# Wider rows for the first loads of queries and keys, and two more pairs of half sums added before the matrix engine

## The chip, the cores and the metric

The kernel runs on one core of a Trainium2 chip. The metric is device time in microseconds (us), the median over the runs. A separate profiled execution gives the trace, whose times count from the start of its span.

Five engines work side by side, each through its own list of instructions in order: PE (TensorE, matmuls; its weight loads are PEld), DVE (VectorE), ACT (ScalarE), POOL (GpSimd) and SP (SyncE, which here issues most DMAs; ACT issues a few). PE writes to `ps`, the accumulation memory of eight banks; everything else lies in `arena`, the on-chip memory that the kernel divides by hand.

## The reference

Attention in which a query sees only keys of its own cluster, then an MLP mixer over tokens and channels (biases and normalisation layers there are none):

```python
# q, k, v: [4, 8, 768, 64]; centroids: [8, 16, 64]
q_assign = argmax(q_n @ c_n.T); k_assign = argmax(k_n @ c_n.T)   # q_n, k_n, c_n: rows of length 1
mask = q_assign[:, :, :, None] == k_assign[:, :, None, :]
scores = where(mask, 0.125 * q @ k.T, -1e9)
attn = softmax(scores) @ v
x = heads side by side: [4, 768, 512]
xt = x.transpose(0, 2, 1)
u = x + (relu(xt @ w_tok1) @ w_tok2).transpose(0, 2, 1)
out = u + relu(u @ w_ch1) @ w_ch2
```

## The kernel before, in words

The 32 (batch, head) problems are worked as 16 pairs of neighbouring heads, pair 0 to pair 15. For a pair m:

- `load_qk` (pairs 0 to 2) brings q and k on chip, `turn_qk` transposes them on PE into a bank and copies them to `Ts[m % 3]`, twelve rows of 128 tokens: rows 0 to 5 keys, 6 to 11 queries, the two heads on partitions 0 to 63 and 64 to 127. For later pairs `load_qkr`, `part_qk` and `join_qk` do it through transposing DMAs.
- `route` multiplies the rows with the normalised centroids (`cbd`), and DVE finds each token's cluster; the result becomes the mask operand. For pair 0 it is placed directly by eight small operations (lines 1116 to 1141), for the others by way of DRAM (`wdm`).
- `scores` gives twelve chunks: two plain matmuls (one per head), two mask matmuls on top of them in the same banks, and ACT's exponential out of the banks. For pair 0 three chunks' plain matmuls are issued ahead.
- `add_up` adds the exponentials of six key blocks on DVE into two half sums `es[0]`, `es[1]`; where `FOLD[m]` is "V", DVE adds these two as well (one 128x1536 add more).
- `values` multiplies exponentials and v, 16 matmuls for each of six blocks. `sums` multiplies the half sums with ones for the denominators: four matmuls for each half, so eight without the fold and four with it. `sums(m - 1)` runs in the values of pair m.

An fp32 matmul that is no transposition runs as two passes, so the trace shows twice as many.

Before pair 0, `begin` loads centroids, queries and keys, lets PE run `BUSY` warming matmuls on the identity, normalises the centroids on DVE (with one square root on ACT), turns the normalised centroids on PE and copies them to `cbd`. ACT then loads the table of the exponential (line 1005).

After the pairs come the token stage and the channel stage of the mixer, in a fast matrix multiplication with seven products in place of eight; its sums of operands and results are adds on DVE and POOL (line 885), and DVE frees the banks that PE writes. The weights of the mixer are rounded by `weight_round` (lines 1380 to 1397, 31 pieces of up to 512 columns, released at `START + STEP * npiece`) and summed on DVE during the pairs and the token stage, and written to DRAM (`wd`, `wdt`) by SP.

What sets the order: PE's instructions stand as the program adds them. All others are put in order ahead of time by `Program.plan`, a list scheduler with a cost for each operation, due times worked back from PE's order, and times before which an operation is not released (`after`); an operation that names two engines (ACT and DVE for copies) goes to the one that the planner finds free earlier. `more` is added to a transfer's planned time to landing.

Of the kernel before, what the change touches and what calls it, by code (L numbers as in the profile page):

```python
# [29 lines left out]
HJ = NJ // 2  # L30
HS = HJ * P
# [18 lines left out]
GRAIN = 32  # L50
BUSY, HITS_AT = 12, 18.0
CHECK_AT = 532.0
FOLD = "-VVVVVVVVVV-----"

# [7 lines left out]
ISSUE = 0.63  # L62
# [7 lines left out]
SELF = 0.13  # L70
START, STEP = 9, 10

# [651 lines left out]
def kernel(  # L724
# [43 lines left out]
    def buf(kb, shape, dt=F32):  # L768
        return Buf(arena, int(kb * 256), shape, dt)
# [15 lines left out]

    qks = [buf(3 + 6 * i, [2, NJ, 2, D]) for i in range(2)]
    vs = [buf(15 + 3 * i, [2, NJ, D]) for i in range(3)]
# [52 lines left out]
    def bank(*i):  # L840
        return [("ps", n) for n in i]
# [58 lines left out]

    def dma(dst, src, rd, wr, kb, row, after=0.0, queue="SP"):

        q = {"SP": nc.sync, "ACT": nc.scalar, "POOL": nc.gpsimd}[queue]
        return g.add(
            {queue: ISSUE}, lambda e: q.dma_start(dst, src), rd, wr, (kb * 1024, row), after  # L905
        )
# [8 lines left out]
    def load_qk(m, after=0.0, queues=("SP", "SP")):  # L915
        b, hp = divmod(m, H // 2)
        t = qks[m % 2]
        for i, a in ((1, k), (0, q)):
            for h, qu in enumerate(queues):
                dma(  # L920
                    t.ap[:, i, :, h],
                    a[b, 2 * hp + h].rearrange("(p j) d -> p j d", p=P),
                    [], [("qk", m % 2, i, h)] + (t.rows(i, i + 1) if h else []), 192, 256,
                    after, qu,
                )

# [19 lines left out]
    def begin():  # L946
        cen, sq = rt[0], rt[1]
        dma(cen.ap[:, 0:D], centroids.rearrange("h c d -> (h c) d"), [], cen.k(), 32, 256)
        load_qk(0, 0.0, ("SP", "ACT"))
        load_qk(1, 1.0)  # L950
# [49 lines left out]

        g.add({"DVE": 4.0}, norm, cen.k(), sq.k() + nsq.k())
        turn_qk(0, (0, 1, 2), (0, 1))
        turn(ps[:, 7, 0:P], sq.ap[:, 0:P], sq.k(), bank(7))
        turn_qk(0, (0, 1, 2), (2,))
        g.add(
# [29 lines left out]

    def turn_qk(m, banks, parts=range(3)):
        src, T = qks[m % 2], Ts[m % 3]
        for n in parts:
            bk = banks[n]
            for i in range(4):  # L1040
                a, j = divmod(4 * n + i, NJ)
                a = 1 - a
                turn(
                    ps[:, bk, i * P : (i + 1) * P],
                    src.ap[:, a, j].rearrange("p h d -> p (h d)"),
                    [("qk", m % 2, a, 0), ("qk", m % 2, a, 1)] + src.rows(a, a + 1), bank(bk),
                )

            copy(
                T.ap[:, 4 * n : 4 * n + 4].rearrange("p a t -> p (a t)"), ps[:, bk], 512,  # L1050
                bank(bk), T.rows(4 * n, 4 * n + 4),
            )

# [107 lines left out]
    def scores(m):  # L1161
# [166 lines left out]
    def pair(m):  # L1328
# [727 lines left out]
```

## Time and profile before

| | us |
|---|---|
| median of 3 runs | 789.43 |
| lowest, highest | 789.1, 789.65 |
| profiled execution | 789.87 |
| its span | 788.0 |

In a line of the timeline stand start, length, engine, line, operation, what it writes and reads, shape and count; in brackets the idle time of the engine before it and what ended it. A group's length runs from its first start to its last end. In the table of stretches stand, for each engine, busy time and count of instructions; behind them the granted clock of PE, the busy share of the 16 DMA engines and what they moved in GB/s. SPq and ACTq are DMA issues. The shape of a copy is partitions x elements.

### The profile page before, as it was taken

What the parts mean: (1) busy time and instruction counts of PE and PEld (TensorE: products, weight loads), DVE (VectorE), ACT (ScalarE), POOL (GpSimd) and SP (SyncE); (2) the same over time, 40 slices, a digit from 0 to 9 for tenths busy, and PEclk for the clock granted to TensorE, in tenths of its full rate; (3) what the DMA queues carried; (4) which work ended last, traced back from release to release, by engine and by line L of the source; (5) the groups of instructions that cost most, each with busy time, mean ns of one, the idle gap of its engine ahead of it and who ended that gap; (6) DMA issues with size and microseconds to landing.
All of it is one profiled execution on the core that took longest, in us unless ns stands there. A gap on an engine that the chain in (4) does not pass through costs nothing.

```text
span 788.0 us, 15324 instructions
## 1 busy us (share of the span) xinstructions
PE 777.8 (99%) x5975; PEld 463.1 (59%) x5975; DVE 675.2 (86%) x848; ACT 461.4 (59%) x614; POOL 194.1 (25%) x187
## 2 busy tenths in 40 slices
PE   8999999999999999999999999999999999999996
PEld 5666666666666666545555555555555555555554
DVE  6979999999998999999999877999853576799964
ACT  5788888889889875599614368633235204400422
POOL 0000000000000000001274598700285289830000
PEclk9999999999999999999999999999999999999999
DMA  9676668876778953568848999975788744444666
GB/s 249 169 192 180 170 154 221 212 202 178 196 196 215 266 178 128 127 135 202 195 124 253 313 281 266 273 189 132 168 189 177 165 100 101 105 105 102 160 164 161
DMA packets 326576, 143.68 MB, mean 182 GB/s; under 512 B 260192, under 2 KB 322400, under 8 KB 326496
## 3 DMA queue, kind: packets, MB, share of 16 engines
q1 hardware_dynamic: 324128, 141.83, 71.6%
q8 instruction: 49, 0.80, 0.4%
q10 hardware_dynamic: 2368, 0.79, 0.4%
q14 instruction: 31, 0.25, 0.1%
HBM read 91.95 MB, written 28.61 MB: 153 GB/s over the span
## 4 chain that ended last, share of the span: by engine, by line
PE 95%; DVE 3%; DMA 1%; issue 0%; ACT 0%; SPq 0%
PE ps L846 77%; PE ps L1238 18%; DVE arena L885 2%; DMA arena<-in_q_dram 1%; DMA arena<-in_moe_w_ch_dram 0%; ACT arena L865 0%; DVE arena L1384 0%; DVE arena L1390 0%; DVE arena L1387 0%; SPq L905 0%; DVE arena L1380 0%; DVE arena L867 0%; ACT arena L1129 0%
## 5 line engine op out<-in xcount | busy, mean ns | idle before, releaser
L846 PE MATMUL ps<-arena 128*128 128x384 f32 (+5 forms) x2727 | 640.2, 463 | 4.5 <-POOL arena masks.py:199 1.4
L846 PEld LDWEIGHTS ps<-arena 128*128 128x128 f32 (+2 forms) x2343 | 340.1, 184 | 250.3 <-issue 61.6
L885 DVE TENSOR_TENSOR arena<-arena 128x1536 f32<-128x1536 f32 (+6 forms) x340 | 369.9, 1109 | 12.5 <-issue 3.6
L885 POOL TENSOR_TENSOR arena<-arena 128x384 f32<-128x384 f32 x181 | 193.4, 1109 | 501.8 <-DVE arena L885 378.6
L885 DVE TENSOR_TENSOR arena<-ps,arena 128x384 f32<-128x384 f32 (+3 forms) x227 | 189.4, 844 | 78.4 <-PE ps L846 76.0
L875 ACT COPY arena<-arena 128x768 uint16<-128x768 uint16 x221 | 189.2, 955 | 62.6 <-DMA arena<-arena 32.8
L1205 ACT ACTIVATE arena<-ps 128x768 f32<-128x768 f32 x192 | 150.7, 811 | 35.2 <-PE ps L846 33.4
L1238 PE MATMUL ps<-arena 128*32 128x192 f32 (+1 forms) x3248 | 144.9, 335 | 0.0
L1238 PEld LDWEIGHTS ps<-arena 128*32 128x32 f32 x3248 | 103.7, 110 | 44.1 <-issue 15.6
L865 ACT COPY arena<-ps 128x512 f32<-128x512 f32 (+2 forms) x44 | 31.3, 719 | 116.1 <-PE ps L846 114.8
L892 ACT ACTIVATE arena<-arena 128x1152 f32<-128x1152 f32 (+1 forms) x38 | 39.7, 1070 | 51.0 <-DVE arena L885 50.3
L1912 ACT ACTIVATE arena<-arena 128x768 f32<-128x768 f32 x40 | 38.7, 969 | 32.8 <-DMA arena<-in_moe_w_ch_dram 27.1
L846 PEld LDWEIGHTS <-arena 64*128 64x128 bf16 x384 | 19.2, 94 | 24.6 <-issue 0.2
L1390 DVE SCALAR_TENSOR_TENSOR arena<-arena 128x512 f32<-128x512 uint32 (+1 forms) x31 | 21.5, 713 | 0.4
L1384 DVE SCALAR_TENSOR_TENSOR arena<-arena 128x512 uint32<-128x512 uint32 (+1 forms) x31 | 20.9, 695 | 0.3
L1108 ACT ACTIVATE arena<-arena 128x384 bf16<-128x384 f32 x16 | 11.2, 701 | 13.6 <-issue 13.6
L1380 DVE TENSOR_SCALAR arena<-arena 128x512 uint32<-128x512 uint32 (+1 forms) x31 | 13.9, 458 | 4.0 <-DMA arena<-in_moe_w_tok_dram 4.0
L1285 DVE STREAM_TRANSPOSE arena<-ps 128x768 f32<-128x768 f32 x16 | 15.2, 952 | 0.4 <-PE ps L1238 0.4
L1387 DVE TENSOR_SCALAR arena<-arena 128x512 uint32<-128x512 uint32 (+1 forms) x31 | 12.8, 436 | 0.4
L1293 DVE STREAM_TRANSPOSE arena<-ps 128x384 f32<-128x384 f32 x16 | 9.3, 579 | 2.2 <-PE ps L1238 2.0
L1098 DVE STREAM_TRANSPOSE arena<-ps 128x384 f32<-128x384 f32 x16 | 9.1, 571 | 1.8 <-PE ps L846 1.8
L1103 DVE STREAM_TRANSPOSE arena<-arena 128x384 f32<-128x384 f32 x16 | 9.3, 578 | 0.6
(57 smaller groups left out, 47.2 us busy)
## 6 DMA issues: line engine op xcount, KB each, us to landing
arena<-wd SPq DMA_DIRECT2D x196, 192.0 KB, 3.0
wd<-arena SPq DMA_DIRECT2D x84, 224.0 KB, 3.0
arena<-in_moe_w_ch_dram SPq DMA_DIRECT2D x96, 128.0 KB, 3.1
arena<-in_moe_w_ch_dram SPq DMA_DIRECT2D x16, 768.0 KB, 5.3
arena<-in_v_dram SPq DMA_DIRECT2D x16, 384.0 KB, 4.8
out_dram<-arena SPq DMA_DIRECT2D x14, 384.0 KB, 3.5
arena<-in_k_dram SPq DMA_DIRECT2D x13, 384.0 KB, 4.2
arena<-in_q_dram SPq DMA_DIRECT2D x13, 384.0 KB, 4.2
```

Source lines behind the costliest of these rows:

```text
L846: nc.tensor.matmul(dst, lhsT=lhsT, rhs=rhs, start=start, stop=stop, tile_position=pos, is_transpose=tr, skip_group_check=True,)
L865: nc.scalar.copy(out=dst, in_=src)
L875: nc.scalar.copy(out=dst, in_=src)
L885: (nc.vector if e == "DVE" else nc.gpsimd).tensor_tensor(out=dst, in0=a, in1=b, op=op)
L892: nc.scalar.activation(out=dst, in_=src, func=ACT.Relu)
L1205: lambda e, ex=ex, s=s, u=u: nc.scalar.activation(out=ex.ap[:, :, u * HS : (u + 1) * HS], in_=ps[:, 2 * s : 2 * s + 2, 0:HS], func=ACT.Exp ...
L1238: nc.tensor.matmul(dst, lhsT=lhsT, rhs=rhs, start=start, stop=stop, tile_position=pos, skip_group_check=True,)
L1285: lambda: nc.vector.transpose(out=x.ap[:, :, cols].rearrange("p j (c d) -> p c j d", d=32), in_=ps[:, 6:8, 0:HS],),
L1380: vec(lambda: nc.vector.tensor_scalar(out=hh, in0=hi, scalar1=0x07FFFFFF, scalar2=3, op0=ALU.bitwise_and, op1=ALU.logical_shift_left,), f, ...
L1384: vec(lambda: nc.vector.scalar_tensor_tensor(out=TT, in0=hi, scalar=0xC0000000, in1=hh, op0=ALU.bitwise_and, op1=ALU.bitwise_or), 0.14 + 0 ...
L1390: vec(lambda: nc.vector.scalar_tensor_tensor(out=ll, in0=lo, scalar=float(2.0**-52), in1=hh.bitcast(F32), op0=ALU.mult, op1=ALU.mult,), 0. ...
L1912: lambda e, i=i, func=func, bias=bias, n=n, hi=hi: nc.scalar.activation(out=hi, in_=hi, func=func, bias=bias, accum_out=wsum.ap[:, i, n : ...
```

## The change

- `load_qk` loads both heads of q, or of k, in one DMA of 384 KB: the layout on chip becomes [q or k, head, row, 64], so that each partition gets 1536 bytes in one piece per head, where it got six pieces of 256 bytes. For pair 0 the keys go by ACT's queue and the queries by SP's; so far each queue had one head of both. The centroids' DMA is issued after the queries on SP.
- `turn_qk` turns two rows of one head at a time (64 values each of token rows 2i and 2i + 1), four parts of three turns in place of three parts of four. Each part is copied by two copies of 64x384 (even rows and odd rows), which put the head on its partitions.
- In pair 0 the first two parts of pair 1 are turned ahead of the three plain chunks, the other two after them.
- `BUSY` from 12 to 9, `START` from 9 to 7, some planned costs (`norm`, the centroids' landing).
- `FOLD`: pairs 11 and 12 get the third add.

In the order that the planner gives the changed kernel, pair 0's eight copies stand seven on ACT and one on DVE, pair 1's six and two, pair 2's five and three; the reduction of line 1019 and its two scalings stand behind the two `cbd` copies, where they stood ahead of them; all else on PE stands as before but for the edits named.

```diff
-BUSY, HITS_AT = 12, 18.0
+BUSY, HITS_AT = 9, 18.0
-FOLD = "-VVVVVVVVVV-----"
+FOLD = "-VVVVVVVVVVVV---"
-START, STEP = 9, 10
+START, STEP = 7, 10
...
-    qks = [buf(3 + 6 * i, [2, NJ, 2, D]) for i in range(2)]
+    qks = [buf(3 + 6 * i, [2, 2, NJ, D]) for i in range(2)]
...
-        for i, a in ((1, k), (0, q)):
-            for h, qu in enumerate(queues):
-                dma(
-                    t.ap[:, i, :, h],
-                    a[b, 2 * hp + h].rearrange("(p j) d -> p j d", p=P),
-                    [], [("qk", m % 2, i, h)] + (t.rows(i, i + 1) if h else []), 192, 256,
-                    after, qu,
-                )
+        for (i, a), qu in zip(((1, k), (0, q)), queues):
+            dma(
+                t.ap[:, i].rearrange("p h j d -> p h (j d)"),
+                a[b, 2 * hp : 2 * hp + 2].rearrange("h (p j) d -> p h (j d)", p=P),
+                [], t.rows(i, i + 1), 384, 1536, after, qu,
+            )
...
-        dma(cen.ap[:, 0:D], centroids.rearrange("h c d -> (h c) d"), [], cen.k(), 32, 256)
-        load_qk(0, 0.0, ("SP", "ACT"))
+        dma(
+            cen.ap[:, 0:D], centroids.rearrange("h c d -> (h c) d"), [], cen.k(), 32, 256,
+            more=-1.7,
+        )
+        load_qk(0, 0.0, ("ACT", "SP"))
...
-        g.add({"DVE": 4.0}, norm, cen.k(), sq.k() + nsq.k())
-        turn_qk(0, (0, 1, 2), (0, 1))
+        g.add({"DVE": 3.0}, norm, cen.k(), sq.k() + nsq.k())
+        turn_qk(0, (0, 1, 2, 4))
         turn(ps[:, 7, 0:P], sq.ap[:, 0:P], sq.k(), bank(7))
-        turn_qk(0, (0, 1, 2), (2,))
...
-    def turn_qk(m, banks, parts=range(3)):
+    def turn_qk(m, banks, parts=range(4)):
...
-            for i in range(4):
-                a, j = divmod(4 * n + i, NJ)
-                a = 1 - a
+            a, h = divmod(n, 2)
+            for i in range(HJ):
                 turn(
                     ps[:, bk, i * P : (i + 1) * P],
-                    src.ap[:, a, j].rearrange("p h d -> p (h d)"),
-                    [("qk", m % 2, a, 0), ("qk", m % 2, a, 1)] + src.rows(a, a + 1), bank(bk),
+                    src.ap[:, 1 - a, h, 2 * i : 2 * i + 2].rearrange("p j d -> p (j d)"),
+                    src.rows(1 - a, 2 - a), bank(bk),
                 )
-            copy(
-                T.ap[:, 4 * n : 4 * n + 4].rearrange("p a t -> p (a t)"), ps[:, bk], 512,
-                bank(bk), T.rows(4 * n, 4 * n + 4),
-            )
+            for j in range(2):
+                copy(
+                    T.ap[D * h : D * h + D, NJ * a + j : NJ * (a + 1) : 2],
+                    ps[D * j : D * j + D, bk, 0:HS].rearrange("p (i t) -> p i t", t=P), HS,
+                    bank(bk), sum((T.rows(NJ * a + i, NJ * a + i + 1) for i in range(j, NJ, 2)), []),
+                )
...
         ahead = 3 if m == 0 else 0
+        if m == 0:
+            turn_qk(1, (7, 6), (0, 1))
         for n in range(ahead):
             plain(n)
         if m == 0:
-            turn_qk(1, (7, 6, 7))
+            turn_qk(1, (0, 0, 7, 6), (2, 3))
...
-                turn_qk(2, (1, 2, 3))
+                turn_qk(2, (1, 2, 3, 4))
```

More of the change, by code (lines that the diff above doesn't have):

```diff
@@ L899, in vec, with dma @@
         return g.add({"DVE": c - 0.08}, lambda e: fn(), rd, wr, after=after, early=early)
-    def dma(dst, src, rd, wr, kb, row, after=0.0, queue="SP"):
+    def dma(dst, src, rd, wr, kb, row, after=0.0, queue="SP", more=0.0):
         q = {"SP": nc.sync, "ACT": nc.scalar, "POOL": nc.gpsimd}[queue]
         return g.add(
-            {queue: ISSUE}, lambda e: q.dma_start(dst, src), rd, wr, (kb * 1024, row), after
+            {queue: ISSUE}, lambda e: q.dma_start(dst, src), rd, wr, (kb * 1024, row), after,
+            more=more,
         )
```

## The prediction

> **What bounds the kernel now.** First the page: its totals, VectorE's (DVE's) busy tenths in 40 slices of 19.7 us, and the chain of waits that ended last.
>
> ```profile
> span 788.0 us, 15324 instructions
> PE 777.8 (99%) x5975; PEld 463.1 (59%) x5975; DVE 675.2 (86%) x848; ACT 461.4 (59%) x614; POOL 194.1 (25%) x187
> DVE  6979999999998999999999877999853576799964
> PE 95%; DVE 3%; DMA 1%; issue 0%; ACT 0%; SPq 0%
> ```
>
> TensorE (PE) is the bound: work taken from it is time, unless something else makes it wait. Only two stretches are not its own. The first is the front; its timeline:
>
> ```profile
> 0.74 0.40 SPq L905 DMA_DIRECT2D arena<-in_centroids_dram  x1
> 1.36 5.20 PE L846 MATMUL ps<-arena 128*128 128x128 f32 x30 [1.36 <-POOL arena masks.py:199]
> 2.60 0.23 DVE L980 TENSOR_TENSOR arena<-arena 128x64 f32<-128x64 f32 x1 [0.28 <-DMA arena<-in_centroids_dram]
> 3.41 0.20 ACT L984 ACTIVATE arena<-arena 128x1 f32<-128x1 f32 x1
> 5.12 0.42 DVE L997 TENSOR_SCALAR arena<-arena 128x64 f32<-128x64 f32 x2
> 6.38 0.59 ACT L865 COPY arena<-ps 128x512 f32<-128x512 f32 x1 [2.77 <-PE ps L846]
> 7.26 0.95 PE L846 MATMUL ps<-arena 128*128 128x128 f32 x7 [0.70 <-DMA arena<-in_q_dram]
> 7.71 1.13 ACT L865 COPY arena<-ps 128x512 f32<-128x512 f32 x2 [0.74 <-PE ps L846]
> 7.82 0.46 DVE L867 COPY arena<-ps 64x64 f32<-64x64 f32 x2 [1.81 <-PE ps L846]
> 8.89 4.14 PE L846 MATMUL ps<-arena 128*32 128x384 f32 x28 [0.68 <-ACT arena L865]
> 12.23 0.97 DVE L1131 TENSOR_SCALAR arena<-arena 32x384 bf16<-32x384 f32 x2
> 13.11 0.51 ACT L1129 CAST arena<-arena 32x384 bf16<-32x384 f32 x1
> 13.23 0.35 DVE L1136 CAST arena<-arena 32x384 bf16<-32x384 f32 x1
> 13.53 1.05 ACT L865 COPY arena<-ps 128x512 f32<-128x512 f32 x2
> 14.62 0.16 PEld L846 LDWEIGHTS ps<-arena 128*32 128x32 f32 x8 [0.50 <-ACT arena L865]
> ```
>
> The 30 passes at 1.36 are 24 of the 12 warming matmuls (two passes each) and six turns of pair 0's keys; at 7.26 come six turns of its queries and the centroids' turn. Route(0) starts at 8.89, the mask's parts are placed from 12.23 to 13.6, route(1) starts at 14.62 behind two copies of pair 1. From there PE has no gap until the second stretch, the token stage, where DVE is the late one:
>
> ```profile
> 381.35 1.73 PE ps L846 x4
> 383.99 0.42 DVE arena L885
> 410.02 371.11 PE ps L846 x1154
> ```
>
> After 410 the chain is PE alone to 781. So the change can act through PE work, the front, and DVE's lateness at 384 to 410.
>
> **Part 1: half sums added for pairs 11 and 12.** The sums of pair m run in pair m + 1. In the chain, pair 11's values (with pair 10's sums, added up on DVE) stand beside those of pair 12, whose sums of pair 11 are not added up:
>
> ```profile
> 236.45 5.98 PE ps L1238 x136
> 255.57 6.63 PE ps L1238 x144
> ```
>
> Eight passes less are 6.63 - 5.98 = 0.65; two pairs (11 and 12): **-1.30 us**, all on the bounding engine.
>
> For it DVE gets two adds of 128x1536:
>
> ```profile
> L885 DVE TENSOR_TENSOR arena<-arena 128x1536 f32<-128x1536 f32 x40 | 69.2, 1747 | 2.1 <-PE ps L1238 0.9 <-ACT arena L1205 0.5
> DVE arena L885 <- issue: 3.3, 1, 3.3
> DVE arena L885 <- PE ps L846: 1.6, 6, 0.4
> PE ps L846 <- DVE arena L885: 1.0, 3, 0.5
> 240.00:260.00 20.00, 16.50 (x28) 1.00 0.87 221
> ```
>
> That is 2 x 1.75 = 3.5 us, in slices where DVE stands at 8 to 9 tenths. Cover: the 3.3 us gap inside 240 to 260, where pair 11's add falls, and 1.6 us in which DVE waits for PE in the token stage. If the cover is gone, weight rounding (lines 1380 to 1390) slips into the token stage and PE's 1.0 us of waits for DVE grows. The planned order of the changed kernel shows such a slip: one rounding's last steps and two sums of 448 (about 0.7 + 2 x 0.6) pass from before to behind the last pair's normalisation; then the orders meet again in the channel stage. PE is also 1.3 us earlier, so DVE has that much less time. Need: 3.5 + 1.3 = 4.8; cover 3.3 + 1.6 = 4.9, but whether the 3.3 us can be filled is not certain (the row names nobody it waited for). Bounds: -1.0 (the waits of now vanish by the new order) to +3.2 (4.8 - 1.6, the gap not fillable). I take **+0.4**: need and cover are about equal, so PE's 1.0 us of waits grow by less than half.
>
> **Part 2: rows of 1536 bytes in the front.** What transfers take now:
>
> ```profile
> arena<-in_v_dram SPq DMA_DIRECT2D x2, 384.0 KB, 4.5
> arena<-in_k_dram SPq DMA_DIRECT2D x3, 192.0 KB, 5.4
> arena<-in_centroids_dram SPq DMA_DIRECT2D x1, 32.0 KB, 1.8
> 1.93 5.20 DMA arena<-in_q_dram
> 7.00:8.00 1.00, 0.74 (x7) 0.75 (x7) 0.18 (x1) 0.29 (x1) 0.00 (x0) 1.00 1.35 218
> 10.00:11.00 1.00, 1.00 (x8) 0.76 (x6) 0.95 (x2) 0.35 (x2) 0.00 (x0) 1.00 1.05 376
> ```
>
> The last column is GB/s: 218 with rows of 256 bytes, 376 when v comes in rows of 1536. Pair 0's keys and queries are 786 KB, on two queues now issued together at 0.74. With the 1.8 us of the small centroid transfer as fixed part, they land at 0.74 + 1.8 + 786/376 = 4.6. Before, the last query lands at 7.13 (1.93 + 5.20), so queries gain 2.5 us. But the centroids, so far first on SP's queue, now stand behind the queries there. They were in use from 2.60; I take 4.8 (33 KB more at the end, and a little for 256-byte rows). Lower bound: issued at about 1.2, with only SP's 393 KB ahead, 1.2 + 1.8 + 1.05 = 4.1; upper: like v's 384 KB in traffic, 1.2 + 4.5 = 5.7. And ACT's square root, which waits for them through DVE, stands ahead of all copies on ACT: that eats the gain:
>
> - square root ends 1.04 after the centroids (2.57, just ahead of 2.60, to 3.61): 5.85. Keys are turned from 5.1 on, so ACT's copies start at 5.9 instead of 6.38.
> - eight copies of 64x384 take the place of three of 128x512 (in the planned order seven on ACT, one on DVE). No row has one: the nearest are 0.51 (32x384) and 0.59 (128x512) long. Three of 128x512 in a row (27.61, below) took 1.57, a pitch of (1.57 - 0.59)/2 = 0.49, and 384/512 of it is 0.37; so between 0.37 and 0.49, and I take 0.4. Seven end at 5.9 + 2.8 = 8.7.
> - the normalised centroids are ready 2.97 after landing (5.54 - 2.57): 7.8; then their turn (0.3), DVE's copy (0.5, ahead of it on DVE) and the two copies of line 867 (0.46): 8.8. The reduction of line 1019 and two scalings (0.5) come after these now, and are done when route(0) is.
> - route(0) at 8.85 to 8.9, against 8.89: nothing gained here.
> - mask: 8.89 to 12.23 is 3.34 of fixed chain; then the first four placements are shared two and two with ACT, 1.0 instead of 1.4. First mask matmuls at about 13.2 instead of 13.85.
> - route(1) needs all eight copies of pair 1. DVE has two, behind placements: 0.49 + 0.35 + 0.5 + 0.49 + 0.5 = 2.3 after 12.2, so 14.5 against 14.62.
>
> Front: **-0.1**; by the bounds of the centroids' landing -0.8 to +0.8. Pair 2 too has eight copies, three of them on DVE ahead of route(2)'s transpose, whose bank pair 1's third chunk waits for:
>
> ```profile
> 27.61 1.57 ACT L865 COPY arena<-ps 128x512 f32<-128x512 f32 x3 [2.76 <-PE ps L846]
> 33.46 0.54 DVE L1098 STREAM_TRANSPOSE arena<-ps 128x384 f32<-128x384 f32 x1
> 34.62 0.36 PEld L846 LDWEIGHTS ps<-arena 64*128 64x128 f32 x4 [0.22 <-issue]
> ```
>
> Slack is 34.62 - 34.0 = 0.6. Three copies of 0.5 come in ahead, a sum of 512 (0.7) passes behind: 0.8 later, so up to 0.2 of wait, and none if DVE is early: **+0.1**.
>
> What this rests on is the order on SP's queue: its 192 KB of keys take 5.4 us though 218 GB/s would move them in 0.9, so transfers wait behind earlier ones. The Trainium skill (DMA: Bandwidth & Descriptors, "Queues, rings and completion order") says a DMA engine consumes one queue's descriptors in ring order; by it the centroids cannot overtake the queries. By the other reading, centroids beside the queries at 1.2 + 1.8 = 3.0, the copies would wait for the turned keys instead, and the front would gain up to the 0.8 of its lower bound.
>
> **Part 3: nine warming matmuls, rounding released 2 us earlier.** The passes, in two cuts of the timeline:
>
> ```profile
> 2.59 2.13 PE L846 MATMUL ps<-arena 128*128 128x128 f32 x9
> 5.29 1.16 PE L846 MATMUL ps<-arena 128*128 128x128 f32 x9
> ```
>
> They come every 0.21 at first ((2.13 - 0.42)/8), and every 0.11 later ((1.16 - 0.27)/8). Six passes less end the warming at about 5.1 instead of 5.7: in time for keys at 4.6 to 5, so it costs nothing; it is what lets copies start before 6. Releasing each weight piece at 7 + 10n rather than 9 + 10n changes nothing in DVE's order up to pair 10 (the planned orders agree); it moves loads on SP that no PE work waits for: 0.
>
> **Sum.** -1.30 + 0.4 - 0.1 + 0.1 = -0.9 us. The profiled execution took 789.87 (span 788.0 and 1.87 around it), 0.44 above the median of 789.43. 789.87 - 0.9 = 788.97; on the median's scale **788.5**. About 0.2% (1.6 us) is what a measurement of this kernel can tell from no change, so this is a small gain inside it.
>
> **Rivals.**
> 1. *Front and token stage both pay.* The centroids land by 4.1 (front -0.8), and the new order takes half of PE's 1.0 us of waits away: -1.3 - 0.8 - 0.5 = -2.6, so 786.8. For it: 376 GB/s beside 218, and a front whose chain is DMA and copies; against: the square root ahead of seven copies.
> 2. *DVE becomes the bound of the token stage.* Place: the sums that free banks from 384 on; price +3.2 with the 3.3 us gap not fillable: -1.3 + 3.2 = +1.9, so 791.3, slower. It decides from the point where more than 1.3 us of DVE's 4.8 find no gap. For it: DVE's nines up to the token stage, three waits of PE; against: DVE still waits 1.6 us for PE just ahead.
> 3. *PE turns slow again.* Between 6.4 and 8.9 PE would have one turn to do, where it has seven passes now. If the 0.21 pace came back at 8.9 for the 3.3 us it lasted at the start, 1.6 us of front work would be added, of which some 0.5 is covered by waits: -0.9 + 1.1 = +0.2, so 789.6. Against: after the idle 0.9 us before 7.26 and 8.89 the pace stayed. The Trainium skill (TensorE: Matmul & The Clock Gate, "Part 1: The HAM clock gate") puts the return at an idle window of about 3.4 us that runs free of the kernel; the gap here is shorter, so by it the pace should stay.
> 4. *The change doesn't do what it says in the front:* queries land early, but route(0) stays at 8.9. That is in the forecast already.
>
> **How the numbers follow.** Forecast 0.47 (own range 787.5 to 789.4), rival 1 0.36, rival 2 0.10, rival 3 0.07. Faster by over 0.2% (below 787.85): nearly all of rival 1 and a small tail of the forecast, 0.39. Slower (above 791.0): most of rival 2 and mishaps beside it, 0.11. The rest, 0.50, within. Range: from just under rival 1, 786.5, to 790.2, past rival 3 and a forecast whose DVE cost is 1.5 higher; rival 2 and the far ends are left out.
>
> **What would show it.** Right: eight passes fewer in the values of pairs 12 and 13; queries landed by 5; first copy on ACT right after the square root; route(0) at 8.6 to 9.2, route(1) at 14.2 to 14.8; PE's waits for DVE at 0.5 to 2 us. Wrong: route(1) before 13.8 or after 15.3, waits of PE for DVE over 3 us or none, a pace of 0.21 after 9 us, or waits in a stage that has none now.

## The result, and the profile after

The changed kernel takes 793.9 us (median of 5 runs, 793.56 to 794.97); the kernel before takes 789.65 beside it (5 runs, 789.1 to 790.87). The ratio is 1.0056, with an interval of 1.0042 to 1.0069: it is slower by 4.3 us, where a gain of 0.9 us was forecast. The range, 786.5 to 790.2, doesn't hold it.

The totals on the page of the changed kernel:

```profile
span 792.5 us, 15269 instructions
PE 778.6 (98%) x5953; PEld 463.6 (59%) x5953; DVE 682.2 (86%) x856; ACT 465.1 (59%) x624; POOL 190.4 (24%) x186
```

Its table of waits, PE's rows (us in total, times, longest):

```profile
PE ps L846 <- DVE arena L867: 2.5, 2, 1.3
PE ps L846 <- DVE arena L885: 2.1, 3, 1.5
PE ps L846 <- DVE arena L999: 1.5, 1, 1.5
```

PE has 22 passes less and works no shorter (778.6 us, 777.8 before); it is the span round it that is longer by 4.5. PE's waits for VectorE come to 6.1 us, on three lines: the sums of line 885, where the kernel before has its only ones, and, new, the copies of line 867 and the normalised centroids of line 999.

To see where the time is lost, take the same five places in the chain of waits of both kernels. Each row gives start, length and line; the rows are route(1) with what follows, the first scores of pair 2, those of pair 13, the work behind the token stage, and the last matmuls. First before:

```profile
14.63 8.32 PE ps L846 x62
52.93 9.89 PE ps L846 x72
285.20 9.89 PE ps L846 x72
410.02 371.11 PE ps L846 x1154
781.76 0.56 PE ps L846 x3
```

and after:

```profile
16.55 8.32 PE ps L846 x62
55.42 9.89 PE ps L846 x72
286.78 9.89 PE ps L846 x72
412.77 15.75 PE ps L846 x48
786.37 0.56 PE ps L846 x3
```

The differences are +1.92, +2.49, +1.58, +2.75 and +4.61. So the front loses 1.92 up to route(1) and 0.57 more up to pair 2; pairs 2 to 13 win 0.91, which is all of the gain by the two adds; the token stage loses 1.17 and the rest, the channel stage, 1.86. In the channel stage no long wait stands behind the 1.86: set matmul by matmul beside the kernel before, PE falls behind in five places, by 0.19, 0.19, 0.56, 0.24 and 0.30 us, at 428.54, 438.48, 506.98, 524.71 and 575.43, and by less than 0.12 at a time elsewhere. So there are two losses, far apart, one in the front and one late, and the experiments take them one by one.

The front of the changed kernel, first a row of the chain of waits, then of the timeline:

```profile
1.24 4.28 DMA arena<-in_centroids_dram
```

```profile
6.25 0.20 ACT L986 ACTIVATE arena<-arena 128x1 f32<-128x1 f32 x1 [3.69 <-DVE arena L985]
6.35 3.27 ACT L865 COPY arena<-ps 64x384 f32<-64x384 f32 x7
8.79 1.03 DVE L867 COPY arena<-ps 64x384 f32<-64x384 f32 x3 [0.41 <-ACT arena L865]
9.97 5.26 PE L846 MATMUL ps<-arena 128*32 128x384 f32 x38 [1.21 <-DVE arena L867]
14.35 0.55 DVE L867 COPY arena<-ps 64x384 f32<-64x384 f32 x1 [0.21 <-PE ps L846]
14.94 0.97 ACT L865 COPY arena<-ps 64x384 f32<-64x384 f32 x2 [0.40 <-DVE arena L867]
15.94 0.56 DVE L867 COPY arena<-ps 64x384 f32<-64x384 f32 x1 [0.53 <-ACT arena L865]
```

The centroids land at 5.52, the square root ends at 6.45, ScalarE copies until 9.6, route(0) starts at 9.97 (8.89 before). Four copies of pair 1 then run one behind the other from 14.35 to 16.5, VectorE, ScalarE twice, VectorE. By the brackets the first waits for PE, and each time the engine changes the next copy waits for the other engine.

### The profile page after: what moved, and what is told of

The parts are those of the page before. It is cut to its first block, busy times and chain, and to the rows that moved or that the text cites. A ratio compares the mean times of both kernels' runs of the same rounds, so it can differ in the third digit from the quotient of the medians.

```text
span 792.5 us, 15269 instructions
## 1 busy us (share of the span) xinstructions
PE 778.6 (98%) x5953; PEld 463.6 (59%) x5953; DVE 682.2 (86%) x856; ACT 465.1 (59%) x624; POOL 190.4 (24%) x186
## 4 chain that ended last, share of the span: by engine, by line
PE 96%; DVE 2%; DMA 1%; ACT 0%; issue 0%; SPq 0%; DVEq 0%
PE ps L846 78%; PE ps L1242 18%; DVE arena L885 2%; DMA arena<-in_centroids_dram 1%; ACT arena L865 0%; DVE arena L867 0%; SPq L905 0%; DVE arena L982 0%; DVE arena L983 0%; ACT arena L986 0%; DVE arena L985 0%; DVE arena L1388 0%; DVEq L885 0%; DVEq L867 0%
## 5 line engine op out<-in xcount | busy, mean ns | idle before, releaser
L885 DVE TENSOR_TENSOR arena<-arena 128x1536 f32<-128x1536 f32 (+6 forms) x343 | 377.1, 1119 | 8.9 <-PE ps L1242 1.4
L885 POOL TENSOR_TENSOR arena<-arena 128x384 f32<-128x384 f32 x180 | 189.7, 1090 | 510.1 <-DVE arena L885 382.1
L865 ACT COPY arena<-ps 64x384 f32<-64x384 f32 (+3 forms) x53 | 34.7, 657 | 114.6 <-PE ps L846 113.2
L1384 DVE TENSOR_SCALAR arena<-arena 128x512 uint32<-128x512 uint32 (+1 forms) x31 | 13.0, 434 | 3.5 <-DMA wdt<-arena 3.5
L1391 DVE TENSOR_SCALAR arena<-arena 128x512 uint32<-128x512 uint32 (+1 forms) x31 | 12.0, 412 | 0.2
L867 DVE COPY arena<-ps 64x384 f32<-64x384 f32 (+3 forms) x15 | 9.2, 617 | 2.7 <-PE ps L846 1.5
```

Source lines behind the costliest of these rows:

```text
L865: nc.scalar.copy(out=dst, in_=src)
L885: (nc.vector if e == "DVE" else nc.gpsimd).tensor_tensor(out=dst, in0=a, in1=b, op=op)
L1384: vec(lambda: nc.vector.tensor_scalar(out=hh, in0=hi, scalar1=0x07FFFFFF, scalar2=3, op0=ALU.bitwise_and, op1=ALU.logical_shift_left,), f, ...
```

## The experiments

All times are medians beside the kernel before, run on the same chip; the ratios are to it, from all runs, and need not be those of the medians. "Ahead" counts the passes of the weight rounding (lines 1380, 1384, 1387 and 1390; 31 pieces, so 124 passes) that stand in VectorE's list ahead of pair 15's transposition of line 1285. The other columns come from the chain of each kernel's profile, as above (e_cen_heads' route(1) from its timeline). One profile is one execution: in the seven kernels that keep the old front route(1) lies between 14.13 and 14.94.

| kernel | ahead | route(1) | pair 2 | pairs 2 to 13 | pair 13 to end of token stage | from there to the last row | median |
|---|---|---|---|---|---|---|---|
| before | 97 | 14.63 | 52.93 | 232.27 | 124.82 | 371.74 | 789.4 to 789.8 |
| changed | 95 | 16.55 | 55.42 | 231.36 | 125.99 | 373.60 | 793.90 |
| e_fold | 95 | 14.13 | 52.43 | 231.37 | 125.96 | 372.93 | 791.08 |
| e_fold11 | 97 | 14.68 | 52.98 | 231.82 | 125.04 | 371.99 | 789.87 |
| e_pool | 94 | 14.20 | 52.50 | 232.95 | 125.94 | 372.94 | 792.24 |
| e_consts | 100 | 14.22 | 52.52 | 232.46 | 125.39 | 371.57 | 789.74 |
| e_start12 | 97 | 14.94 | 53.25 | 231.56 | 125.04 | 373.12 | 789.32 |
| e_after5 | 97 | 16.66 | 55.82 | 231.56 | 125.06 | 371.99 | 793.53 |
| e_fold11s7 | 100 | 14.72 | 53.02 | 232.01 | 125.40 | 372.34 | 790.47 |
| e_front | 97 | 18.18 | 57.04 | 232.08 | 124.79 | 371.75 | 792.24 |
| e_cen | 95 | 17.98 | 56.83 | 231.37 | 125.97 | 373.46 | 793.64 |
| e_cen_heads | 96 | 17.30 | 56.31 | 231.56 | 125.07 | 372.00 | 792.49 |
| e_ch10 | 97 | 16.81 | 56.80 | 232.08 | 124.79 | 371.74 | 791.63 |
| e_warm | 97 | 15.77 | 54.70 | 232.07 | 124.79 | 371.75 | 792.53 |
| e_split | 100 | 19.68 | 57.98 | 232.50 | 125.37 | 371.57 | 795.52 |
| e_twice | 100 | 17.57 | 55.87 | 232.50 | 125.35 | 371.57 | 793.91 |

### The late loss

**e_fold**: the kernel before with the two adds and nothing else.

```diff
-FOLD = "-VVVVVVVVVV-----"
+FOLD = "-VVVVVVVVVVVV---"
```

> The kernel before with the fold for pairs 11 and 12 alone. Theory A (the late loss, 1.2 us in the token stage and 1.9 us in the channel stage, belongs to the two adds on DVE): eight passes less in pairs 12 and 13 each (-1.3 us), but the gaps of PE around 384 to 413 and 500 to 575 come back, so +1 to +2 us against before. Theory B (it comes from the other edits, which shift the planned order): -1.3 +- 0.4 us, no new gap behind 412.

791.08 us, ratio 1.0023 (1.0013 to 1.0032). The two adds alone make the kernel slower: by the table they win 0.90 in pairs 2 to 13 and lose 1.14 and 1.19 behind them, together +1.43, and the medians differ by 1.49. The timeline of e_fold, and below it that of the kernel before, at the end of the token stage:

```profile
409.76 1.56 PE L846 MATMUL ps<-arena 128*128 128x384 f32 x4 [1.47 <-DVE arena L885]
```

```profile
410.02 1.24 PE L846 MATMUL ps<-arena 128*128 128x384 f32 x3 [0.48 <-DVE arena L885]
```

PE waits 1.47 there for a sum of VectorE, where it waited 0.48. Was VectorE overfull in pairs 11 to 13? The table of stretches has busy time and count of PE, PEld, DVE, ACT and POOL; its row for 240 to 300 us before, and the row of line 1390 in the groups of that stretch:

```profile
240.00:300.00 60.00, 60.00 (x888) 37.61 (x884) 55.45 (x82) 45.62 (x60) 0.00 (x0) 1.00 0.78 217
```

```profile
L1390 DVE SCALAR_TENSOR_TENSOR arena<-arena 128x512 f32<-128x512 uint32 x6 | 3.9, 685 | 0.0
```

and the same two rows of e_fold:

```profile
240.00:300.00 60.00, 60.00 (x896) 37.69 (x892) 58.61 (x81) 44.24 (x59) 0.00 (x0) 1.00 0.71 199
```

```profile
L1390 DVE SCALAR_TENSOR_TENSOR arena<-arena 128x512 f32<-128x512 uint32 x4 | 2.6, 685 | 0.0
```

VectorE's busy time rises by 3.16 us, so its idle time was filled; still two of six passes of line 1390 (and two of line 1387) have left the stretch, as the groups by line in the same stretch show. They are done later, and in the end two more passes are left for the time behind pair 15 (95 of 124 ahead, where it was 97). There they are dear. Two rows of the kernel before show it, from the token stage, where the same passes that take 0.42 us (line 1387) and 0.69 us (line 1390) in 240 to 300 take 1.11 and 1.37:

```profile
405.46 1.11 DVE L1387 TENSOR_SCALAR arena<-arena 128x512 uint32<-128x512 uint32 x1
406.60 1.37 DVE L1390 SCALAR_TENSOR_TENSOR arena<-arena 128x512 f32<-128x512 uint32 x1
```

GpSimd adds beside them there (20 of 128x384 between 380 and 420) and does nothing in 240 to 300; that this is the reason was not tested. In the channel stage e_fold falls behind in four of the five places of the changed kernel, by the same 0.19, 0.19, 0.24 and 0.30.

**e_fold11**: one add instead of two (`FOLD = "-VVVVVVVVVVV----"`).

> The kernel before with eleven pairs folded: one add of 1.75 us more on VectorE, 0.65 us of TensorE less. Theory A (VectorE's spare time in 240 to 300 us is 4.3 us before and 0.7 us with two adds, and what does not fit is pushed late): one add still fits, the gap before 410 stays at 0.5 us as in the kernel before, and the time is 788.7 to 789.4. Rival (each add is paid late whatever its number): 790.2 to 790.6, half of the loss of 1.5 us with two adds.

789.87, ratio 0.9999 (0.9990 to 1.0008): no loss, and no gain either. With one add 97 passes stay ahead; the token stage loses 0.22 and the channel stage 0.25, as much as the 0.45 that the fold wins in pairs 2 to 13 (0.65 was expected). So the steep loss comes with the second add, as the theory has it, but its gain doesn't.

**e_pool**: two adds, those of pairs 11 and 12 on GpSimd.

```diff
-FOLD = "-VVVVVVVVVV-----"
+FOLD = "-VVVVVVVVVVPP---"
...
-        if FOLD[m] == "V":
-            tt(a.ap, a.ap, b.ap, ALU.add, 2 * S, a.k() + b.k(), a.k())
+        if FOLD[m] in "VP":
+            tt(
+                a.ap, a.ap, b.ap, ALU.add, 2 * S, a.k() + b.k(), a.k(),
+                ("DVE",) if FOLD[m] == "V" else ("POOL",),
+            )
```

> The kernel before with twelve pairs folded, the add of pairs 11 and 12 on GpSimd in place of VectorE. Theory A (what costs is VectorE's time: two adds of 1.75 us push mask work out of pairs 11 and 12 into the token stage): were GpSimd's add free to VectorE, the time would be 788.1 to 788.7. A GpSimd add of 128x384 takes 1.14 us in the token stage and VectorE's instructions on SBUF alone take about twice their time beside it there (384 elements 1.11 for 0.55 us, L1387 1.11 for 0.42), so this add of four times the size takes some 4.5 us and takes 1.8 to 2.3 us from VectorE: by that the gain is lost again and the time is 790.5 to 792, with the gap of about 2 us before 410 still there. Rival B (the sums come too late for TensorE in pairs 11 and 12): TensorE's waits stand in those pairs, 790 to 793.

792.24, ratio 1.0033 (1.0021 to 1.0045). The timelines of GpSimd, VectorE and PE in pair 11:

```profile
242.41 3.51 POOL L885 TENSOR_TENSOR arena<-arena 128x1536 f32<-128x1536 f32 x1 [241.11 <-DVE arena L885]
238.75 7.46 DVE L885 TENSOR_TENSOR arena<-arena 128x1536 f32<-128x1536 f32 x4
246.75 3.50 PE L846 MATMUL ps<-arena 64*128 64x384 f32 x24 [1.50 <-DVE arena L1098]
```

The add costs VectorE 0.46 us here (four adds in 7.46, against 4 x 1.75), not the 1.8 to 2.3 expected, but a transposition behind these adds comes late and PE waits 1.5. And the late loss is whole (125.94, 372.94) although the adds are off VectorE, which is busy for 56.07 of the 60 us from 240 to 300: 94 passes stand ahead. So what is paid late is not the adds' time on VectorE; it goes with the place that the planner gives to the rounding.

**e_start12**: two adds, and `START` 7 on the kernel before, which by the planned order puts the passes back to 97.

```diff
-FOLD = "-VVVVVVVVVV-----"
+FOLD = "-VVVVVVVVVVVV---"
-START, STEP = 9, 10
+START, STEP = 7, 10
```

> The kernel before with twelve pairs folded and START 7. Of the 124 VectorE passes that turn weights into their working form, 97 stand ahead of the end of pair 15 in the program before, 95 with twelve pairs alone (and 95 in the changed kernel, 94 with the adds on GpSimd), and 97 again with START 7 here. Theory A2 (what is paid late are the conversion passes that the two adds push behind pair 15 into the token stage): the gap of 1.95 us at 408 shrinks to 1.0 or less, the gaps at 425, 435, 520 and 571 go, and the time is 788.3 to 789.1. The rival (VectorE's total time counts, wherever the passes stand): 790.6 to 791.5 as with twelve pairs alone.

789.32 beside 789.44, ratio 0.9995 (0.9986 to 1.0004); e_fold's interval lies wholly above it. Chain of e_start12:

```profile
53.25 9.89 PE ps L846 x72
284.81 9.89 PE ps L846 x72
409.85 48.92 PE ps L846 x150
500.13 282.19 PE ps L846 x878
```

The token stage takes 125.04 us with the same two adds that made it 125.96. The time is above the 788.3 to 789.1 expected; the fold wins 0.71 in this profile and not 1.3. The 373.12 in the channel stage holds a pause of 0.75 us ahead of 500.13, behind an add of GpSimd. That execution took 791.07, the longest of eleven, and e_after5, with the same folds and 97 passes too, doesn't have the pause.

**e_after5**: the changed kernel with `START` 5 (`-START, STEP = 7, 10` / `+START, STEP = 5, 10`).

> The changed kernel with START 5 in place of 7, by which 97 conversion passes stand ahead of the end of pair 15 instead of 95. Theory A2: the late loss of some 2.4 us goes in good part and the loss of the front stays: 791.0 to 792.3. The rival (place of the passes does not count): 793.4 to 794.4 as the changed kernel.

793.53, ratio 1.0057 (1.0038 to 1.0076) from four runs between 792.32 and 795.72. The median misses what was expected; the profile doesn't: 125.06 and 371.99 in place of 125.99 and 373.60, so the late loss is down from 3.0 us to 0.5, and of the five places in the channel stage none is left. The spread of the runs goes with the clock (below): their mean granted clock is 0.998, 0.997, 0.996 and 0.994, in the order of their times. The run at 0.998 took 792.32; five runs of the changed kernel, all at 0.998 or 0.999, took 793.56 or more.

**e_consts**: the kernel before with `BUSY` 9 and `START` 7.

> The kernel before with BUSY 9 and START 7 alone, so three idle matmuls less at the start and the late store's pieces due 2 us earlier. Theory: neither counts, 789.3 to 789.9, granted clock 1.00 in all slices up to 20 us. Rival (three warming matmuls less let TensorE's clock fall in the front, as it did in profiles of the new front): 790.5 to 792 with slices at 0.50.

789.74, ratio 1.0000 (0.9991 to 1.0009). Without the adds and the new front the two constants together cost nothing that can be seen.

**e_fold11s7**: one add and `START` 7.

> The kernel before with eleven pairs folded and START 7: 100 of the 124 conversion passes stand ahead of the end of pair 15, three more than in the kernel before. Theory A2 (what is late in the token stage is set by the passes left over): pairs 2 to 13 gain 0.45 us as with eleven pairs alone and the stretch from pair 13 to 410 us takes no longer than the 124.82 us of the kernel before; time 788.7 to 789.3. The rival (VectorE's total time counts as well): 789.5 to 790.0, as with eleven pairs alone.

790.47, by the medians 0.9 us more than the kernel before; the ratio, 1.0003 (0.9980 to 1.0025), says little, since one run of the kernel before took 797.57 then. Both expectations fail: with 100 passes ahead the token stage takes 125.40, longer than with 97. The columns of the table show the same in all sixteen kernels: 124.79 to 125.07 with 96 or 97 passes, 125.35 to 125.40 with 100, 125.94 to 125.99 with 94 or 95. Why more passes ahead make it longer wasn't found. So the count alone isn't the rule; that it matters which pieces stand where is a guess.

### The front

**e_front**: the change without the two adds and with `START` 9.

> The changed kernel with FOLD for ten pairs and START 9, as before: only the wide rows, the new turns and copies, and nine warming matmuls are left. All theories: route(1) starts at 16.5 as in the changed kernel and pair 2 begins 2.5 us later than before. Theory A: the late stages are as before, so +2.5 us against before. Theory B: a late loss is here too, +3 to +5 us.

792.24, ratio 1.0035 (1.0021 to 1.0049). The token and the channel stage take what they take before (124.79, 371.75), so the two losses are independent, as theory A has it. Pair 2 starts 4.1 us late in its profile, more than the changed kernel's 2.5; that run took 793.65 with a mean clock of 0.996, and the clock fell in it (below). The three runs at 0.998 took 791.91 to 792.24, some 2.5 us more than the kernel before.

**e_cen**: the changed kernel with the centroids issued first on SP again, ahead of the queries (the queries are released 0.05 later).

```diff
-        load_qk(0, 0.0, ("ACT", "SP"))
+        load_qk(0, 0.0, ("ACT", "SP"), 0.05)
```

> The changed kernel with the centroids' transfer issued first on SP again, ahead of pair 0's queries. If the late centroids (5.5 in place of 2.6) set the front: square root done by 3.7, ACT's copies start at 5.5 in place of 6.4, route(0) at 9.0 to 9.3 in place of 9.97, route(1) 0.8 earlier. Rival (copies of the interleaved rows that wait for each other across ACT and DVE set route(1)): route(0) moves, but route(1) comes 1.5 us or more after its masks, no earlier than 16.0.

793.64, ratio 1.0044 (1.0027 to 1.0060). Route(0) starts at 9.78, 0.2 sooner than in the changed kernel and not at the 9.0 to 9.3 expected, and the time is the same within the intervals. Its profile is that of its longest run (795.42), in which the clock fell; in the table of stretches PE's granted clock stands behind POOL:

```profile
10.00:11.00 1.00, 1.00 (x10) 0.44 (x3) 0.53 (x3) 0.40 (x2) 0.00 (x0) 0.79 1.05 392
11.00:12.00 1.00, 1.00 (x6) 0.70 (x4) 0.93 (x3) 0.49 (x2) 0.00 (x0) 0.50 1.07 393
12.00:13.00 1.00, 1.00 (x5) 0.67 (x6) 0.97 (x2) 0.96 (x3) 0.00 (x0) 0.50 1.05 401
13.00:14.00 1.00, 1.00 (x6) 0.52 (x4) 0.88 (x3) 0.97 (x2) 0.00 (x0) 0.50 0.44 172
14.00:15.00 1.00, 1.00 (x8) 0.38 (x4) 0.00 (x0) 0.67 (x2) 0.00 (x0) 1.00 0.08 31
```

From 10.6 to 14.0 PE runs at half its clock, and the 29 passes behind the start of route(0) take 5.91 us in its chain, where they take 4.28 in the changed kernel. Without these 1.63 us route(1) would start at 16.35 in place of 17.98 (an estimate), 0.2 ahead of the changed kernel's 16.55. So the late centroids are worth some 0.2 us here, and the rival's sign, route(1) no earlier than 16.0, holds. The three other runs, with a mean clock of 0.999, took 792.19 to 793.69. Half a clock stands also in the profiles of e_front, e_cen_heads, e_split and, from 17.8, e_ch10; in those of the kernel before and of the changed kernel all slices up to 35 us are at 1.00.

**e_cen_heads**: e_cen, and each copy bound to an engine by its head, so that even and odd rows of one head no longer cross engines.

```diff
+                    (("ACT",), ("DVE",))[h],
```

> As the run before, and the copies of turn_qk bound to engines by head: head 0 on ACT, head 1 on DVE, so that the even and the odd rows of one head never stand on two engines. If the waits between ACT and DVE make the rest of the front's loss: no copy waits for the other engine, route(0) at 8.3 to 9.0, route(1) at 14 to 14.8, pair 2 within 0.4 us of before. Rival (the count of copies, 24 in place of 9, is what costs): route(1) stays past 15.5.

792.49, ratio 1.0030 (1.0018 to 1.0043), just under the changed kernel's interval. Route(0) starts at 9.34 and route(1) at 17.30, later than the theory has it, in a profile with the clock at half from 9.3 to 12.7. Such a fall costs some 1.6 us (below), so the rival's sign, route(1) past 15.5, holds by little. The late stages take 125.07 and 372.00, though this kernel has both adds and `START` 7: 96 passes stand ahead of pair 15 here, one more than in the changed kernel, and the late loss is down to 0.5. It is this, and not the front, that is seen to be better.

**e_warm**: e_cen_heads with ten pairs, `START` 9, and five idle matmuls behind the centroids' transposition.

```diff
+        keep_busy(5, sq.k())
```

> The new keys' and queries' layout with ten pairs added on VectorE and START 9, the centroids' transfer first on SP's queue again, the copies of one head all on one engine, and five more idle 128x128 matmuls behind the transpose of the centroids, so that TensorE does not stand still for 2 us before route(0). The theory (TensorE stood idle for 2.15 us ahead of route(0) in the version before it, its granted clock fell to 0.50 from 9.6 to 12.3 us there, and this was luck of the run): the granted clock stays 1.00 in every slice up to 20 us, route(0) starts at 9.2 to 9.5, route(1) before 15.8, and the time is 789.6 to 790.6 with little spread. The rival (the clock falls whatever TensorE does then, or it was not the clock): slices at 0.50 stay and the time is 791 to 792.5.

792.53, ratio 1.0032 (1.0021 to 1.0043). The profiled run has the clock at 1.00 in all slices from 3 to 25 us, starts route(0) at 8.73, and took 791.11; two of seven runs have 0.996 and took 793.1. So five matmuls don't keep the clock up in all runs. The five other runs took 790.96 to 792.57, above the 789.6 to 790.6 expected: where the clock is up 1.2 us or more are still lost. Route(1) is at 15.77, 1.1 later than before, though route(0) starts earlier than before.

**e_ch10**: e_cen_heads with ten pairs and `START` 9, without the idle matmuls.

> The new layout with the centroids' transfer first on SP's queue, copies of one head on one engine, ten pairs folded and START 9: all that has been found put right in the front but the idle matmuls of e_warm. Theory C: the eight half copies still cost the front, 790.2 to 791.5 in runs whose granted clock stays up, 1.5 us more in runs where it falls. The rival (the crossed waits and the centroids were the whole loss): 788.8 to 789.8.

791.63, ratio 1.0035 (1.0022 to 1.0047). Four runs at 0.998 took 791.35 to 791.63, about the upper end of what was expected; two at 0.996 took 792.88 and 793.27, some 1.6 us more, and one at 0.997 took 794.82. VectorE's copies and route(1) in its timeline:

```profile
12.47 1.12 DVE L867 COPY arena<-ps 64x384 f32<-64x384 f32 x2
14.08 0.96 ACT L865 COPY arena<-ps 64x384 f32<-64x384 f32 x2 [1.98 <-PE ps L846]
15.63 1.12 DVE L867 COPY arena<-ps 64x384 f32<-64x384 f32 x2
16.81 5.49 PE L846 MATMUL ps<-arena 128*32 128x384 f32 x28 [0.51 <-DVE arena L867]
```

No copy waits for another engine's copy any more, the clock is full up to 17.8, and route(1) is not earlier than the changed kernel's 16.55: VectorE now has 2.2 us of copies amid the mask work that route(1) needs. So binding the copies by head ends the crossed waits and not the delay. A front with neither the crossed waits nor half of the copies on VectorE wasn't run.

**e_split**: the kernel before with each 128x512 copy made as two of 64x512, one on each engine.

> The kernel before (its transfers, its transposes, its constants) with each copy of 128x512 out of PSUM for the first three pairs made as two of 64x512, one on ScalarE and one on VectorE. Theory C (the front of the changed kernel is late because eight copies of half the partitions take the place of three whole ones): six copies in place of three, of 0.59 us each by the whole ones' row, are 1.8 us more engine time a pair, about 0.9 on each of two engines; route(0) 0.2 to 0.8 us later than 8.89, route(1) 0.6 to 1.5 us later than 14.6, and the time 790.2 to 791.6. The rival (it is the late landing of the centroids and the crossed waits of even and odd rows, not the number of copies): 789.3 to 789.9.

795.52, ratio 1.0074 (1.0055 to 1.0094), far over either theory. It is no clean test: the two halves brought crossed waits of their own (route(0) waited 2.54 us for VectorE), and the clock was at half from 11.7 to 15.1.

**e_twice**: the kernel before with each of its nine copies made twice on ScalarE; the second writes the same values once more.

```diff
-            copy(
+            for _ in range(2):
+                copy(
...
-                bank(bk), T.rows(4 * n, 4 * n + 4),
-            )
+                    bank(bk), T.rows(4 * n, 4 * n + 4), ("ACT",),
+                )
```

> The kernel before with each of the nine 128x512 copies of the first three pairs made twice on ScalarE, and nothing else; the second write of the same values waits only for ScalarE itself, so no wait crosses engines. Theory C (the copies' engine time sets the front): three more copies of 0.57 us ahead of route(0), less 0.74 us in which ScalarE stood idle between the first two, put route(0) 0.9 to 1.7 us later than 8.89, and the next pair's three put route(1) 0.9 to 2.5 us later than 14.63; time 790.5 to 792.5. By theory D (TensorE's clock falls where TensorE has stood still for some 2 us ahead of route(0), in some runs and whatever the layout) some runs have a mean granted clock of 0.996 or less and are about 1.5 us longer than the others, and a profile of such a run shows slices at 0.50 between 9 and 14 us. The rival (copies are hidden; only the crossed waits and the centroids made the new front late): 789.2 to 789.9.

793.91, ratio 1.0048 (1.0025 to 1.0071). Its timeline:

```profile
6.79 3.53 ACT L865 COPY arena<-ps 128x512 f32<-128x512 f32 x6 [3.17 <-PE ps L846]
10.37 4.13 PE L846 MATMUL ps<-arena 128*32 128x384 f32 x28 [2.34 <-ACT arena L865]
15.36 1.25 PE L846 MATMUL ps<-arena 128*128 128x128 f32 x10 [0.86 <-ACT arena L865]
17.57 1.70 PE L846 MATMUL ps<-arena 128*32 128x384 f32 x12 [0.96 <-ACT arena L865]
```

Route(0) is 1.48 late and route(1) 2.94, with transfers, layout and centroids as before: copies alone can put the front late, here by more than in the changed kernel. And the falls of the clock are not the new layout's alone: five of ten runs stand at 0.998 to 1.000 and took 792.8 to 793.3, five at 0.995 to 0.997 and took 794.5 to 795.1.

## Why the prediction was wrong, point by point

By the chain the four terms of the sum came to -0.91, +3.03, +1.92 and +0.57, in all +4.6 in the profile, where -1.30, +0.4, -0.1 and +0.1 were forecast. Two of them carry the miss: the price of the adds on VectorE, and the front up to route(1).

- **The bound** was right: PE, the front and the token stage. "From there PE has no gap until the second stretch, the token stage" held; the channel stage, which it left out, lost 1.86.
- **Part 1, -1.30**: the passes went as said (values of 5.98 us in place of 6.63), but the scores in the same stretch took 10.09 instead of 9.89 in both pairs, so that 0.91 was won; why the scores take longer wasn't found. The later runs have it in the same size: 0.45 for one pair, 0.71 to 0.91 for two.
- **Part 1, +0.4**: this is the step that failed first, and by most: 3.03 us were lost. It set a need of 4.8 us against 4.9 us of idle time of VectorE and took filled idle time as cover. It was fillable, and was filled (3.16 of 3.5 in 240 to 300), and the loss came all the same: 1.17 in the token stage and 1.19 to 1.86 behind it. The text had seen the slip in the planned order ("one rounding's last steps ... pass from before to behind") and priced it at little; with the slip undone by `START` the same adds cost 0.5 (e_after5; e_start12's time agrees), and without `START`, in e_cen_heads, too; with the adds off VectorE but the slip kept (e_pool) the loss stayed. "Then the orders meet again in the channel stage" was no reason for no cost there.
- **Part 2, -0.1 up to route(1)**: +1.92. Three terms of the sum were too small. The centroids landed at 5.52 instead of 4.8, behind the queries on SP as assumed, near the upper bound of 5.7 (that they "cannot" overtake doesn't follow from the order in which descriptors are taken up, and one order of issue doesn't show it). A copy of 64x384 took 0.47 in ScalarE's row, at a pitch of (3.27 - 0.47) / 6 = 0.47 and not 0.4: no part of it overlapped. With 0.6 from the square root and 6 x 0.07 from the pitch route(0) comes 1.0 later, and it came at 9.97 for 8.87. From there to route(1) 5.6 us were reckoned and 6.58 were needed. The copies of pair 1 were taken as side work of VectorE between placements, from 12.2 on. But the rows for the last four weren't turned then. In the chain PE works from route(0) on for longer than before, because two parts of pair 1 are now turned ahead of the three plain chunks; the row before and the row after:

```profile
8.89 3.71 PE ps L846 x24
```

```profile
9.97 4.28 PE ps L846 x29
```

Only at 14.35 did the four copies begin, and then they ran one behind the other. The wait that ends last is thus one for PE and then for a row of copies, and not the placing of the mask. What the turns' new place costs by itself wasn't run. Nor were the copies set against those before as a whole: 8 x 0.47 is 3.8 us of two engines a pair, where it was 3 x 0.59 = 1.8. e_twice and e_ch10 show that copies of such a length can set the start of route(1).

- **Part 2, +0.1 for route(2)**: +0.57 between route(1) and pair 2, same sign, too small.
- **Part 3, 0**: right (e_consts). But `START` isn't idle beside the adds: it is what can put the rounding back.
- **Rival 1** (faster, 0.36) rested on a front that wins by early transfers; the queries did land early and nothing waited for them.
- **Rival 2** (slower, 0.10) is near what happened: rounding that slips behind the pairs. But its condition, a gap that can't be filled, didn't hold, and of the loss 1.17 lies in the token stage, its place, and 1.86 in the channel stage, which it doesn't name. That its price of 3.2 us is near the 3.03 is luck.
- **Rival 3** (PE slow again, 0.07) didn't happen in the five runs of the changed kernel (clock 0.998 and 0.999), but it is real in this front. e_front, with the same transfers, layout and copies, has two of five runs at 0.996, and e_after5 has two of four at 0.996 and 0.994; a fall costs some 1.6 us by e_ch10's and e_twice's runs. That the changed kernel's runs were spared is luck as far as the runs show.
- Of the signs, the eight passes fewer, the queries by 5 (issued at 0.74, 4.3 us to landing) and the first copy right behind the square root came. Route(0) at 9.97 missed its 8.6 to 9.2. Of the signs named as wrong, route(1) after 15.3, waits of PE for VectorE over 3 us (6.1) and waits in a stage that has none now came.

## What to carry to other kernels

Where a list is planned ahead, price an addition by what it pushes behind the next full stretch, in the planned order, and not by the idle time that it fits into; here a release time 2 us earlier undid most of the late loss, and none of the versions tried beat the kernel before. Before a layout is changed for the transfers' sake, add up what it asks of the engines that empty the accumulation banks: rows that leave half the partitions of each copy unused more than doubled that work (3.8 us for 1.8) in the one stretch where it sets the start. And ask when the rows of a copy are ready, not only which engine is free for it. A front in which PE has to wait can pay twice, by the wait and, in some runs, by the clock (e_front in two of five runs, e_twice in five of ten).

## What the runs showed of the hardware that was not expected

- A copy of half the partitions costs ScalarE as much as one of all. Its copy of 64x512 in the timeline of e_split takes 0.58 us, where that of 128x512 took 0.59:

```profile
6.44 0.58 ACT L865 COPY arena<-ps 64x512 f32<-64x512 f32 x1 [2.82 <-PE ps L846]
```

- Each fall of the clock is of one length. In e_cen's stretches above it is 0.21 / 0.5 + 3 = 3.42 us at 0.50. In e_front it is 0.45 / 0.5 + 2 + 0.26 / 0.5 = 3.42 as well (the two stretches left out are at 0.50). The three other profiles with a fall, e_cen_heads, e_split and e_ch10, give 3.38 to 3.42. Timeline and stretches of e_front:

```profile
5.70 1.85 PE L846 MATMUL ps<-arena 128*128 128x128 f32 x11
8.47 0.33 PE L846 MATMUL ps<-arena 128*128 128x128 f32 x1 [0.92 <-DVE arena L999]
10.01 6.78 PE L846 MATMUL ps<-arena 128*32 128x384 f32 x38 [1.21 <-DVE arena L867]
```

```profile
10.00:11.00 1.00, 0.99 (x8) 0.18 (x8) 0.42 (x3) 0.99 (x2) 0.00 (x0) 0.55 1.14 335
...
13.00:14.00 1.00, 1.00 (x6) 0.65 (x8) 0.93 (x3) 0.96 (x3) 0.00 (x0) 0.74 0.07 29
```

The Trainium skill (TensorE: Matmul & The Clock Gate, "Part 1: The HAM clock gate (the "warmup" mystery)") gives the window by which the clock is set as about 3.4 us, free of the kernel's own time, and the length agrees. It puts a fall behind a whole idle window; here, in e_front, PE stood still for 0.92 + 1.21 = 2.13 us, with one transposition of 0.33 between. The same page ("Part 4: PE-mode transpose") says that transposing matmuls don't count as busy in the same way; what stands between the warming matmuls and route(0) is transpositions alone, so by that the idle time is longer. No run here separates the two. In e_ch10 the measurement differs from the whole idle window: of the 3.4 us ahead of its fall at 17.8 PE is busy for 1.8 (0.80 from 15.50 on with mask matmuls, 1.0 from 16.81 on with route(1)), and the clock falls all the same.

- The falls stand on a grid that the kernel doesn't set. PE's passes in the front come every 0.21 us at first and every 0.11 later, and each fall begins a whole number of times 3.4 us behind that change of pace: once in e_front (6.70 to 10.10), e_cen (7.18 to 10.58) and e_cen_heads (5.86 to 9.25), twice in e_split (4.89 to 11.70), three times in e_ch10 (7.58 to 17.82). Where the grid lies differs from profile to profile: the change of pace comes at 4.6 to 7.6 us, with the first matmul at 1.36 in each. So it is chance, as far as these profiles show, how a pause of PE lies on the grid. Standing still by itself doesn't decide: in the changed kernel's profile PE stands still for 1.46 + 1.21 = 2.67 us ahead of route(0) with the clock up, and none of its five runs has a mean clock under 0.998.
